# Turning k by a DMA transfer instead of TensorE, in a fused attention and MoE kernel

## The chip, the cores and the metric

The kernel runs on one core of one Trainium2 chip. The metric is the device time of one execution in microseconds (us); lower is better. Times of a kernel are given as the median of several runs with the lowest and highest.

## What is computed

Attention with a softmax that has one more term in its sum, over 8 batches, 12 heads, 448 rows and 64 columns of a head, and behind it a two-layer network with the Mish function on 3584 rows of 768:

```python
batch, n_heads, seq, head_dim = (8, 12, 448, 64)
n_tokens, d_model, d_ff = (3584, 768, 2048)

scores = scale * np.matmul(q, k.transpose(0, 1, 3, 2))
m = np.max(scores, axis=-1, keepdims=True)
e = np.exp(scores - m)
attn = e / (np.sum(e, axis=-1, keepdims=True) + np.exp(-m) + 1e-09)
attn_out = np.matmul(attn, v)
x = attn_out.transpose(0, 2, 1, 3).reshape(B * S, H * D)
h = x @ w_in
sp = np.where(h > 20.0, h, np.log1p(np.exp(np.minimum(h, 20.0))))
out = (h * np.tanh(sp)) @ w_out
```

All inputs and the output are float32 in HBM. The kernel multiplies in bfloat16.

## The kernel before

**Tiling.** Two heads of a batch make a pair, so there are 48 pairs, six a batch. Three pairs make a unit (`UNIT_PAIRS = 3`), and two units a batch. One pair takes 448 rows of q, k and v, held as 112 partitions times 4 rows (`SP_ = 112`, `NT = 4`).

**A pair's path.** `load_pair` (L121) brings q, k and v of a pair into float32 tiles, each by a transfer of 224 KB on the queue of SP (L128); each of the three has three buffers. `cast_pair` (L165) turns q and k into bfloat16 on GpSimd (L179, L180), `cast_v` (L185) does so for v (L188). `transpose_pair` (L190) turns q and k with TensorE: four transposes of 112x128 each for q and for k (L208), into two PSUM banks of a score tile. `evac_qk` (L221) copies them to SBUF: VectorE writes the scaled q in a block-diagonal tile `qd` in two halves (L254), ScalarE copies k to `kT` (L262). `scores` (L291) multiplies `qd` and `kT` into one of three score tiles (L311), and VectorE takes the row maximum `negm` (L332). `exps` (L337) runs the exponentials on ScalarE into `en` (L345). `denominators` (L363) and `normalise` (L410) scale `en` on VectorE (L414, seven a pair) and then turn it by one DMA transpose a pair on the queue of SP into `eT` (L422): 128 partitions times 28 blocks of 128 columns, 896 KiB. `av_pair` (L445) multiplies `eT` with v (L462), three pairs later than the pair's scores. A few early pairs have part of this turned by TensorE instead (L434).

**The network.** `mm1_mish` (L493) is one of 16 column blocks of the first layer for a batch: six matmuls (L498) and a Mish on ScalarE (L504). `mm2_part` (L523) makes parts of the second layer (L551), with a copy to `o_sb` on VectorE (L534) and stores on the queue of SP (L516).

**The order of the work.** It is written out by hand: each engine runs its instructions in program order, and so does the queue of SP. After six pairs done one by one (L618 to 651), the loop at L653 goes through the units, from u = 2. A unit has two stretches. The first (L664 to 717) has twelve steps: the exponentials of a step, a piece of the second layer as filler for TensorE, the scores ahead of it, and the AV product of the unit before at the end of each pair. At steps 0, 3 and 6 (`LOAD_AT`) it calls loads and casts:

```python
load_pair(at + LEAD, "qk")       # LEAD = 4 pairs ahead
load_pair(at + 1, "v")
cast_pair(at + LEAD - 1, with_v=False)
cast_v(at)
```

The second stretch (L724 to 746) has eight blocks f of the first layer. At f = 0 the unit's first pair is normalised and turned, at f = 3 and f = 7 the other two. At f = 1, 3 and 5 q and k of the next unit's three pairs are turned and copied (L740, L741). At f = 4, 6 and 7 the next unit's first scores are computed (L738, L743).

Loads, stores and the DMA transposes of `en` share the queue of SP, in program order: a unit's nine loads and its stores, then its three transposes. Each transfer also waits until the eighth transfer ahead of it on this queue has landed.

Of the kernel before, what the change touches and what calls it, by code (L numbers as in the profile page):

```python
# [10 lines left out]
BF16 = mybir.dt.bfloat16  # L11
# [4 lines left out]
UNIT_PAIRS = 3  # L16
# [3 lines left out]
def kernel(  # L20
# [9 lines left out]
    nc = tc.nc  # L30

    B, H, S, D = q.shape
# [3 lines left out]
    NT = 4  # L36
    SP_ = S // NT
    HP = H // 2
# [9 lines left out]
    N_PAIRS = B * HP  # L48
# [4 lines left out]
    def pool(name, bufs, space=None):  # L53
        if space is None:
            return ctx.enter_context(tc.tile_pool(name=name, bufs=bufs))
        return ctx.enter_context(tc.tile_pool(name=name, bufs=bufs, space=space))
# [2 lines left out]
    singles = pool("singles", 1)  # L59
    ld_pool = pool("ld", 3)  # L60
    bf_pool = pool("bf", 4)
    qk_pool = pool("qk", 3)
    st_pool = pool("st", 5)
    hl_pool = pool("hl", 4)
    rb_pool = pool("rb", 2)
# [38 lines left out]
    loaded, casted, qkT, att, xT, o_sbs, stats = {}, {}, {}, {}, {}, {}, {}  # L104
# [60 lines left out]
    def cast_pair(p, with_v=True):  # L165
        if p >= N_PAIRS:
            return
        q_f, k_f, v_f = (loaded[p].get(nm) for nm in "qkv")
        q_bf = bf_pool.tile([SP_, NT, 2, D], BF16, tag="q_bf", name="q_bf")
        k_bf = bf_pool.tile([SP_, NT, 2, D], BF16, tag="k_bf", name="k_bf")  # L170
        v_bf = bf_pool.tile([SP_, 2, NT * D], BF16, tag="v_bf", name="v_bf", bufs=12)
        by_t = "p h (t d) -> p t h d"
        q_t, k_t = (t.rearrange(by_t, t=NT) for t in (q_f, k_f))
        if p == 0:
            nc.vector.tensor_copy(out=k_bf, in_=k_t)
            for half in (slice(0, NT // 2), slice(NT // 2, NT)):
                nc.vector.tensor_copy(out=q_bf[:, half], in_=q_t[:, half])
        else:
            nc.gpsimd.tensor_copy(out=q_bf, in_=q_t)  # L179
            nc.gpsimd.tensor_copy(out=k_bf, in_=k_t)  # L180
        casted[p] = (q_bf, k_bf, v_bf)
        if with_v:
            cast_v(p)

    def cast_v(p):  # L185
        if p >= N_PAIRS:
            return
        nc.gpsimd.tensor_copy(out=casted[p][2], in_=loaded.pop(p)["v"])  # L188

    def transpose_pair(p, bank=None):  # L190
        if p >= N_PAIRS:
            return
        q_bf, k_bf, _ = casted[p]
        if bank is None:
            ps = mo_take()
            ps_k = mo_take() if p == 0 else ps
        else:
            ps, ps_k = sc_tiles[2 - bank][:, 0, :], sc_tiles[2 - bank][:, 1, :]
        by_s = [
            t[:, :].bitcast(BF16).rearrange("p (s n) -> p s n", s=2)[:, s, :]  # L200
            for s, t in enumerate((ps, ps_k))
        ]
        by_2 = sc_tiles[2][:, 0, :].bitcast(BF16)
        srcs = list(enumerate((q_bf, k_bf)))
        for s, src in reversed(srcs) if p == 0 else srcs:
            for t in range(NT):
                to = by_2 if p == 0 and s == 0 and t >= NT // 2 else by_s[s]
                nc.tensor.transpose(  # L208
                    to[:, t * SP_ : (t + 1) * SP_],
                    src[:, t].rearrange("p h d -> p (h d)"),  # L210
                    ident[:SP_, :SP_],
                )
        own = [] if bank is not None else [ps, ps_k] if p == 0 else [ps]
        qkT[p] = (by_s, own)
# [6 lines left out]
    def evac_qk(p, act=False):  # L221
        if p >= N_PAIRS:
            return
        (q_ps, k_ps), own = qkT[p]
        mo_free.extend(own)
        q_reads = []
        qd = q_diag[p % 3]
        kT = qk_pool.tile([128, S], BF16, tag="kT", name="kT")
        if p < DIAG_FROM:
            qT = qd.rearrange("d i h r -> d (i h r)")[:, 0:S]  # L230
            qkT[p] = (qT, kT)
            if p == 0:
                nc.scalar.copy(kT, k_ps[:, 0:S])
                by_2 = sc_tiles[2][:, 0, :].bitcast(BF16)
                for ps, half in (q_ps, slice(0, S // 2)), (by_2, slice(S // 2, S)):
                    nc.vector.tensor_scalar(
                        out=qT[:, half], in0=ps[:, half], scalar1=SCALE, scalar2=None,
                        op0=ALU.mult,
                    )
                return  # L240
            if act:
                nc.scalar.mul(qT, q_ps[:, 0:S], SCALE)
            else:
                q_reads.append(nc.vector.tensor_scalar(
                    out=qT, in0=q_ps[:, 0:S], scalar1=SCALE, scalar2=None, op0=ALU.mult
                ))
        else:
            qkT[p] = (qd, kT)
            if p < DIAG_FROM + 3:
                nc.vector.memset(qd[0:64, :, 1, :], 0.0)  # L250
                nc.vector.memset(qd[64:128, :, 0, :], 0.0)
            for h in range(2):
                rows = slice(64 * h, 64 * h + 64)
                q_reads.append(nc.vector.tensor_scalar(  # L254
                    out=qd[rows, :, h, :],
                    in0=q_ps[rows, 0:S].rearrange("d (i r) -> d i r", i=QB),
                    scalar1=SCALE, scalar2=None, op0=ALU.mult,
                ))
        if own and not act:
            nc.vector.tensor_copy(out=kT, in_=k_ps[:, 0:S])  # L260
        else:
            k_read = nc.scalar.copy(kT, k_ps[:, 0:S])  # L262
            if not own:
                apart(k_read, *q_reads)
# [145 lines left out]
    def normalise(p, dma=True):  # L410
# [9 lines left out]
        if dma:  # L420
            n = NT - 1 if p < HEAD else NT
            nc.sync.dma_start_transpose(  # L422
# [168 lines left out]
    LEAD = UNIT_PAIRS + 1  # L591
    LOAD_AT = (0, 3, 6)
    HEAD = HP

    BY_PE = {HEAD - 1: 1, HEAD: -2, HEAD + 1: 2}
    AV_AT = {0: {1: 3, 5: 4, 8: 5}, 1: {1: 8, 4: 6, 8: 7}}
# [20 lines left out]

    for p in range(HEAD):  # L618
        for s in range(STEPS):
# [33 lines left out]
    for u in range(UNITS_PER_B, N_UNITS + 2 * UNITS_PER_B):  # L653
# [10 lines left out]
        for n in range(steps):  # L664
            pi, s = divmod(n, STEPS)
            p, idx = p0 + pi, p0 * STEPS + n
            late_tp = u == UNITS_PER_B and n == STEPS
            exps(idx)
            if u == UNITS_PER_B + 1 and n == 0:
                for j in range(2):  # L670
                    turn_on_pe(HEAD, j, busy_first=3)
            flush_late()
            if late_tp:
                transpose_pair(p0 + 2)
                evac_qk(p0 + 2)
            if held and n == 1:
                late.extend(held)
                held.clear()
                flush_late()
            late.extend(slow)  # L680
            slow.clear()
            acc += weight[n]
            want = int(total * acc / sum(weight) + 1e-6)
            while done < want:
                fn, w = filler.popleft()
                fn()
                done += w
            scores_ahead(end)
            if n in LOAD_AT:
                at = p0 + LOAD_AT.index(n)  # L690
                load_pair(at + LEAD, "qk")
                load_pair(at + 1, "v")
                cast_pair(at + LEAD - 1, with_v=False)
                cast_v(at)
            for pe, n0 in BY_PE.items():
                j = n - n0
                first = 2 if pe == HEAD else 0
                if pe // UNIT_PAIRS == u - 1 < first_mm2 - 1 and first <= j < NT:
                    turn_on_pe(pe, j, busy_first=1)
            spread = RDEN_AT.get(u - UNITS_PER_B, {})  # L700
            if n in spread:
                on_act = u < first_mm2
                spread_rden(
                    spread[n], copy=nc.scalar.copy if on_act else nc.vector.tensor_copy,
                    behind=slow if on_act else late,
                )
            early = AV_AT.get(u - UNITS_PER_B)
            if early is not None and n == 7:
                keep_busy(6, bank=mo_free[0])
            if early is not None:  # L710
                if n in early:
                    av_pair(early[n], half=p)
            elif s == (2 if pi else 0) and N_PAIRS <= p < N_PAIRS + UNIT_PAIRS:
                av_pair(p - UNIT_PAIRS)
            if u - UNITS_PER_B < len(W_AT):
                at = (u - UNITS_PER_B, n)
                load_w(W_AT[at[0]].get(n, 0), behind=W_BEHIND.get(at))
# [6 lines left out]
        for f in range(FF_U):  # L724
# [19 lines left out]
            if f in (3, FF_U - 1) and p0 >= LATE_DIV:  # L744
                p = todo[1 + f // (FF_U - 1)]
# [33 lines left out]
```

## Time and profile before

| | |
|---|---|
| three runs, median (lowest to highest) | 480.35 us (479.74 to 483.63) |
| the profiled execution, its own time | 479.66 us |
| its span, first to last instruction | 477.9 us |
| granted TensorE clock, mean | 0.996 |
| busy: TensorE, VectorE, ScalarE, GpSimd | 458.8, 358.7, 344.7, 103.8 us |
| k turned by TensorE, all pairs | 192 transposes; ScalarE's copies of it at L262 from score tiles 20.8 us, 39 of 534 ns |
| DMA transposes of `en` | 45, median 6.7 us from issue to landing |
| loads of k | 48, median 5.2 us from issue to landing |

A busy time is the union of an engine's instructions; matmuls overlap in the array, so the time that one of them adds is the distance between two starts and not its own duration. A name such as "PE mo L551" is engine, tile written and source line. The rows of the DMA issues are those of the queue in which SP stands; the duration of such a row is how long SP was held by the issue, and the landing is told apart from it. SP has no row in the busy times.

### The profile page before, as it was taken

How to read it: one execution, taken by the hardware profiler on the slowest of the kernel's cores; microseconds unless marked ns; L12 is line 12 of the kernel's file. 1: busy time of each engine (PE TensorE's matmuls, PEld its weight loads, DVE VectorE, ACT ScalarE, POOL GpSimd, SP SyncE). 2: the span in 40 equal slices, each digit the busy share in tenths (PEclk: the TensorE clock that was granted, in tenths of full speed). 3: DMA queues.
4: the chain of work that ended last, by engine and by line, in shares of the span. 5: the costliest groups of instructions: out<-in, count | busy, mean ns of one | idle time of the engine just before them, and what ended most of it. 6: DMA issues, size and time to landing. Idle time of an engine off the chain costs nothing.

```text
span 477.9 us, 9363 instructions
## 1 busy us (share of the span) xinstructions
PE 458.8 (96%) x3291; PEld 257.8 (54%) x3291; DVE 358.7 (75%) x715; ACT 344.7 (72%) x907; POOL 103.8 (22%) x186
## 2 busy tenths in 40 slices
PE   6878999999999999999999999999999999999996
PEld 3344555555555565556555555555555555556563
DVE  5899849569898998889899979888898889421011
ACT  5998878788797868788787968687887978312300
POOL 3623536106031311304040312204040300000000
PEclk9999999999999999999999999999999999999999
DMA  8999999999999979898989999989989596961122
GB/s 215 227 224 213 234 222 183 185 212 233 195 301 207 261 149 214 211 198 227 192 229 171 267 156 260 198 192 231 190 220 198 173 181 156 156 142 34 34 63 71
DMA packets 204975, 91.09 MB, mean 191 GB/s; under 512 B 161792, under 2 KB 201472, under 8 KB 204928
## 3 DMA queue, kind: packets, MB, share of 16 engines
q1 hardware_dynamic: 197408, 84.18, 81.0%
q0 software_dynamic: 7488, 6.29, 8.8%
q8 instruction: 26, 0.43, 0.4%
q14 instruction: 21, 0.17, 0.1%
q10 hardware_dynamic: 32, 0.02, 0.0%
HBM read 45.61 MB, written 11.01 MB: 118 GB/s over the span
## 4 chain that ended last, share of the span: by engine, by line
PE 69%; DVE 8%; ACT 6%; issue 1%; DVEq 0%
PE mo L498 24%; PE mo L551 24%; PE sc L311 7%; ACT en L345 6%; PE sc L462 6%; DVE negm L332 5%; PE sc L498 3%; PE sc L208 3%; DVE en L414 1%; DVE xT L475 1%; PE mo L462 1%; DVE o_sb L534 1%; PE mo L272 0%; DVE eT L437 0%; ACT L345 0%
## 5 line engine op out<-in xcount | busy, mean ns | idle before, releaser
L345 ACT ACTIVATE en<-sc,negm 128x448 bf16<-128x448 f32 x336 | 208.7, 640 | 22.5 <-DVE negm L332 20.7
L332 DVE TENSOR_REDUCE negm<-sc 128x2 f32<-128x896 f32 x192 | 182.6, 970 | 39.6 <-PE sc L311 29.3
L551 PE MATMUL mo<-w_out_sb,gT 128*128 128x384 bf16 (+1 forms) x1024 | 166.8, 307 | 0.4 <-DVE rb L402 0.4
L498 PE MATMUL mo<-xT,w_in_sb 128*128 128x448 bf16 x672 | 141.9, 353 | 0.3 <-DVE xT L475 0.3
L551 PEld LDWEIGHTS <-gT 128*128 128x128 bf16 x1024 | 96.3, 98 | 56.0 <-issue 1.9
L504 ACT ACTIVATE gT<-mo 128x448 bf16<-128x448 f32 x112 | 59.3, 543 | 78.9 <-PE mo L498 78.6
L498 PEld LDWEIGHTS <-w_in_sb 128*128 128x128 bf16 x768 | 72.7, 98 | 63.4 <-issue 3.2
L179 POOL CAST q_bf<-q_f 112x512 bf16<-112x512 f32 x47 | 29.9, 635 | 222.1 <-DMA q_f<-in_q_dram 196.1
L414 DVE TENSOR_SCALAR en<-en,rden 128x448 bf16<-128x448 bf16 x252 | 74.2, 367 | 0.8
L311 PE MATMUL sc<-kT,qd 128*128 128x448 bf16 x252 | 71.6, 354 | 0.1
L345 ACT ACTIVATION_READ_ACCUMULATOR en<-sc,negm 128x1 f32 x336 | 71.0, 211 | 0.0
L534 DVE COPY o_sb<-mo 128x384 f32<-128x384 f32 (+1 forms) x64 | 31.8, 497 | 48.3 <-PE mo L551 48.1
L462 PE MATMUL sc<-eT,v_bf 112*64 112x448 bf16 x336 | 39.8, 357 | 1.4 <-ACT en L345 0.9
L311 PEld LDWEIGHTS <-qd 128*128 128x128 bf16 x252 | 24.4, 97 | 29.0 <-issue 12.9
L188 POOL CAST v_bf<-v_f 112x512 bf16<-112x512 f32 x48 | 29.9, 624 | 31.5 <-DMA v_f<-in_v_dram 31.4
L254 DVE TENSOR_SCALAR qd<-sc 64x448 bf16<-64x448 bf16 x72 | 27.7, 385 | 6.2 <-PE sc L208 5.4
L462 PEld LDWEIGHTS <-v_bf 112*64 112x64 bf16 x384 | 20.0, 109 | 20.0 <-issue 11.6
L180 POOL CAST k_bf<-k_f 112x512 bf16<-112x512 f32 x47 | 29.2, 622 | 6.1 <-DMA k_f<-in_k_dram 3.5
L262 ACT COPY kT<-sc 128x448 bf16<-128x448 bf16 x39 | 20.8, 534 | 0.6 <-PE sc L208 0.6
L498 PE MATMUL sc<-xT,w_in_sb 128*128 128x448 bf16 x96 | 20.8, 353 | 0.0
L475 DVE CAST xT<-sc 128x448 bf16<-128x448 f32 x33 | 20.3, 614 | 0.0
L208 PEld LDWEIGHTS <-q_bf 112*128 112x128 bf16 x192 | 13.7, 99 | 10.0 <-POOL q_bf L179 2.0
(61 smaller groups left out, 278.9 us busy)
## 6 DMA issues: line engine op xcount, KB each, us to landing
k_f<-in_k_dram SPq DMA_DIRECT2D x48, 224.0 KB, 5.2
q_f<-in_q_dram SPq DMA_DIRECT2D x48, 224.0 KB, 5.2
v_f<-in_v_dram SPq DMA_DIRECT2D x48, 224.0 KB, 5.5
w_in_sb<-in_moe_w_in_dram POOLq DMA_DIRECT2D x12, 256.0 KB, 8.7
w_out_sb<-in_moe_w_out_dram POOLq DMA_DIRECT2D x8, 384.0 KB, 10.1
out_dram<-o_sb SPq DMA_DIRECT2D x7, 336.0 KB, 3.7
out_dram<-o_sb SPq DMA_DIRECT2D x8, 288.0 KB, 4.8
out_dram<-o_sb SPq DMA_DIRECT2D x8, 240.0 KB, 3.4
```

The source lines that it names most:

```text
L179: nc.gpsimd.tensor_copy(out=q_bf, in_=q_t)
L180: nc.gpsimd.tensor_copy(out=k_bf, in_=k_t)
L188: nc.gpsimd.tensor_copy(out=casted[p][2], in_=loaded.pop(p)["v"])
L311: nc.tensor.matmul(sc[:, bk, 0:S], lhsT=qT[:, i].rearrange("d h r -> d (h r)"), rhs=kT, start=True, stop=True,)
L332: half_max[p] = nc.vector.tensor_reduce(out=negm, in_=sc[:, 0 : len(cols), 0:S], axis=AX.X, op=ALU.max, negate=True)
L345: e = nc.scalar.activation(out=st["en"][:, :, c, 0:SP_], in_=sc[:, bk, 0:S].rearrange("q (j c) -> q j c", j=NT), func=AF.Exp, bias=st["neg ...
L414: nc.vector.tensor_scalar(out=en[:, :, i, 0:SP_], in0=en[:, :, i, 0:SP_], scalar1=st["rden"][:, i : i + 1], scalar2=None, op0=ALU.mult,)
L462: mm = nc.tensor.matmul(av[h * 64 : (h + 1) * 64, 0:S], lhsT=v_bf[:, h, j * D : (j + 1) * D], rhs=e_h, start=(j == 0), stop=(j == NT - 1),)
L498: nc.tensor.matmul(h_ps[:, 0:S], lhsT=w_in_sb[:, dm, ff * 128 : (ff + 1) * 128], rhs=xT[b][:, dm, :], start=(dm == 0), stop=(dm == DM_T - 1),)
L504: nc.scalar.activation(out=gT[:, ff, b % 2 * S : b % 2 * S + S], in_=h_ps[:, 0:S], func=AF.Mish)
L534: nc.vector.tensor_copy(out=o_sb[:, cols.start : cols.start + n_dve], in_=st["o"][:, 0:n_dve])
L551: nc.tensor.matmul(st["o"][:, 0:n_cols], lhsT=gT[:, ff, i * 128 : (i + 1) * 128], rhs=w_out_sb[:, ff, cols], start=(ff == 0), stop=(ff == ...
```

## The change

From pair 15 on (`K_BY_DMA_FROM = 2 * HP + UNIT_PAIRS`), k is turned by a DMA transpose on the queue of SP. It is issued right behind the cast of that pair's k in the order of the program, so between the loads of the unit before: behind the three loads of steps 0, 3 and 6, once each. It reads the cast tile (112 partitions times 512) and writes `kT` (128 partitions times 4 blocks of 112), which the scores read. TensorE then turns q alone for these 33 pairs (15 to 47), and ScalarE makes no copy for them. `kT` gets six buffers where it had three. The tile of v's cast is taken when v is cast instead of when q and k are, and has eight buffers where it had twelve. By the two programs' orders, TensorE has 132 transposes and their weight loads fewer, ScalarE 33 copies fewer, the queue of SP 33 transfers more; VectorE and GpSimd have the same instructions in the same order.

```diff
-    qk_pool = pool("qk", 3)
+    qk_pool = pool("qk", 6)
...
-        q_f, k_f, v_f = (loaded[p].get(nm) for nm in "qkv")
+        q_f, k_f = (loaded[p][nm] for nm in "qk")
...
-        v_bf = bf_pool.tile([SP_, 2, NT * D], BF16, tag="v_bf", name="v_bf", bufs=12)
...
-        casted[p] = (q_bf, k_bf, v_bf)
+        casted[p] = [q_bf, k_bf, None]
...
-        nc.gpsimd.tensor_copy(out=casted[p][2], in_=loaded.pop(p)["v"])
+        v_bf = bf_pool.tile([SP_, 2, NT * D], BF16, tag="v_bf", name="v_bf", bufs=8)
+        nc.gpsimd.tensor_copy(out=v_bf, in_=loaded.pop(p)["v"])
+        casted[p][2] = v_bf
+
+    kT_ahead = {}
+
+    def turn_k_by_dma(p):
+        if not K_BY_DMA_FROM <= p < N_PAIRS:
+            return
+        kT_ahead[p] = qk_pool.tile([128, S], BF16, tag="kT", name="kT")
+        nc.sync.dma_start_transpose(
+            out=kT_ahead[p].rearrange("d (t p) -> d t p", t=NT),
+            in_=casted[p][1].rearrange("p t h d -> p (t h d)"),
+        )
...
-        srcs = list(enumerate((q_bf, k_bf)))
+        srcs = list(enumerate((q_bf, k_bf)))[: 1 if p in kT_ahead else 2]
...
-        kT = qk_pool.tile([128, S], BF16, tag="kT", name="kT")
+        kT = kT_ahead.pop(p, None)
+        by_dma = kT is not None
+        if not by_dma:
+            kT = qk_pool.tile([128, S], BF16, tag="kT", name="kT")
...
+        if by_dma:
+            return
         if own and not act:
             nc.vector.tensor_copy(out=kT, in_=k_ps[:, 0:S])
         else:
...
+    K_BY_DMA_FROM = 2 * HP + UNIT_PAIRS
...
                 cast_pair(at + LEAD - 1, with_v=False)
+                turn_k_by_dma(at + LEAD - 1)
                 cast_v(at)
```

## The prediction, made before the changed kernel ran

> **What bounds the kernel now.** I read the page's busy times first, then the chain that ended last, then one period of the unit loop in sums per stretch, then the timelines of TensorE and SP inside it.
>
> ```profile
> PE 458.8 (96%) x3291; PEld 257.8 (54%) x3291; DVE 358.7 (75%) x715; ACT 344.7 (72%) x907; POOL 103.8 (22%) x186
> ...
> PE 69%; DVE 8%; ACT 6%; issue 1%; DVEq 0%
> ```
>
> TensorE works for 96% of the span and carries 69% of the chain. The first AV products of successive units start at 153.2, 179.7, 206.2, 232.8, 259.2 and so on to 391.8, so a unit takes 26.5 us. Two such periods in sums (columns: length, then busy time and instructions of TensorE, weight loads, VectorE, ScalarE, GpSimd, then clock, DMA share, GB/s):
>
> ```profile
> 206.20:232.80 26.60, 26.50 (x192) 15.63 (x193) 23.66 (x49) 21.56 (x57) 5.62 (x9) 1.00 0.95 212
> 232.80:259.20 26.40, 26.40 (x174) 14.31 (x173) 23.80 (x48) 21.48 (x57) 5.44 (x9) 1.00 0.91 207
> ```
>
> TensorE has no idle time in a period, at full clock; VectorE needs 23.2 of it in the mean over nine periods, ScalarE 21.5. So inside the loop time is worth what it takes from TensorE. The chain in order of time, in the stretch of the first layer, says what the transposes take there (start, us, what):
>
> ```profile
> 248.46 1.14 PE mo L498 x6
> 249.59 0.40 PE sc L208 x8
> 249.99 1.14 PE mo L498 x6
> 251.12 0.38 PE sc L311 x2
> ```
>
> Eight transposes (four of q, four of k) hold the chain for 0.40 us between two groups of matmuls. TensorE's timeline of a later unit shows the halves: k's start 0.20 us behind q's, and the next matmul 0.20 us behind k's. Each row's 0.36 us is mostly overlap.
>
> ```profile
> 273.27 0.36 PE L208 MATMUL sc<-ident,q_bf 112*128 112x112 bf16 x4
> 273.47 0.36 PE L208 MATMUL sc<-ident,k_bf 112*128 112x112 bf16 x4
> 273.67 1.30 PE L498 MATMUL sc<-xT,w_in_sb 128*128 128x448 bf16 x6
> ```
>
> **Removed.** 33 pairs times 0.20 us of TensorE is 6.6 us, all on the path as long as TensorE has no idle time: 0.6 us in each of 11 units (those whose second stretch turns pairs 15 to 47). It cannot be more than the rows' union of 0.36 us a pair, 11.9 us, and I take 0.20 because the distance of starts is what the next instruction sees. The 33 copies of ScalarE at 534 ns are 17.6 us, and worth nothing: in that stretch ScalarE waits for TensorE (the waits have 78.6 us of Mish at L504 behind L498), and a period would have to fall from 26.5 to about 21 before ScalarE bound it.
>
> **Added on the queue of SP.** 33 transposes, each 112x512 bfloat16 = 112 KiB, an eighth of a transpose of `en` (896 KiB). The rows for the price of an issue:
>
> ```profile
> L422 SPq DMA_TRANSPOSE eT<-en x31: 4099/4246/5017, 127.8 to 391.6; - x31
> ...
> DMA to landing us min/median/max: 6.1/6.6/8.4
> ```
>
> (ns, fewest, median, most). An eighth of 4.25 is 0.53; with the semaphore I take 0.6 us. From below, the issue of a plain load of 224 KB holds SP 0.41 us. From above: in the first 50 us the transposes of 21 blocks held SP at least 4.02 us, hardly less than 28 blocks, so a fixed cost near 4 us is not excluded by durations alone. What speaks for the eighth is that bytes flow at a steady 216 to 218 GB/s during an issue (the windows 252 to 253 and 254 to 255 us), and 896 KiB at that rate are 4.2 us: SP is held as long as the bytes take. The 21-block ones ran beside weight loads.
>
> SP's own time in a period is visible in its timeline:
>
> ```profile
> 196.24 14.65 SPq L422 DMA_TRANSPOSE eT<-en  x3
> 211.00 0.98 SPq L516 DMA_DIRECT2D out_dram<-o_sb  x2
> ...
> 217.17 1.80 SPq L516 DMA_DIRECT2D out_dram<-o_sb  x2
> 222.96 4.13 SPq L422 DMA_TRANSPOSE eT<-en  x1
> ```
>
> Over 196.24 to 222.96 the issues of three transposes (13.1), nine loads and four stores add up to 18.7 us, semaphores 0.3; SP waits for the other 7.7, and 5.6 to 8.1 in the steady periods. Into this go three issues (1.8 us) and the waits for casts. The first `kT` of a unit finds its k cast long ago. The second waits for a k whose load was issued three issues earlier: in the unit at 264, that k's cast ends at 269.4, where SP would stand at about 267.9, so 1.5 us; the third about 0.5 us. Behind these waits stand the next loads, the stores and the next unit's three transposes of `en`. In all 3.8 us of 7.4 (6.8 when a period is 0.6 shorter): it fits, and costs 0. On the page of the Trainium skill "VectorE: DVE Perf Modes", section "The three transpose paths", a 128x128 transpose is given as 390 ns on TensorE and 1309 ns by DMA, and its section "Rules for kernel authors" says to use TensorE if PSUM may take the result. By these figures four blocks would be an estimated 5.2 us of DMA against 1.6 us of TensorE, and the change would lose. The trace differs from both: 28 blocks in 4.25 us are 152 ns a block, and a transpose on TensorE adds 50 ns.
>
> **Added on the DMA engines.** 112 KiB at 217 GB/s are 0.53 us, at the 290 GB/s seen in other windows 0.40. From above, add the spread of the landings of `en`'s transposes, 8.4 less 6.1, for transposes that meet other traffic: 2.8 us. I take 1.0, near the lower end, as 0.53 plus half a microsecond for each change from copies to a transpose and back. Three a period are 3 us. The cover: the DMA engines stand still before a unit's first transpose of `en` (0.00 in the windows 249 to 251 and 275 to 276, 1 to 2 us), and each such transpose flows at SP's 218 GB/s where 290 is possible, 1.0 us of reserve each. That is about 4.5 us. What is late next is `eT`: it lands 1.9 to 5.2 us before its AV product in the steady units, median 3.4 (the transpose issued at 254.55 lands at 260.6, its AV starts at 264.2). Only in the first changed unit is there less: issue 123.40, landing 131.4, AV 131.6, with weight loads in the queue. There I put 0.5 us of stall (bounds 0 and 1.5).
>
> **Moved waits.** `qd` on VectorE does not get faster: TensorE reaches the scores at f = 4 0.4 us earlier and those at f = 7 0.6 us earlier. In 9 of 11 units `qd` is ready 0.4 to 1.9 us ahead. In two it is not (118.40 and here), and there the 0.6 us are lost:
>
> ```profile
> 250.89 0.17 PEld L311 LDWEIGHTS <-qd 128*128 128x128 bf16 x2 [0.20 <-DVE qd L254]
> ```
>
> Two times 0.6 is 1.2 us back (bounds 0, and 6.6 if VectorE holds every unit). `kT` itself is issued near 266.5 in this unit and read at 277.5; no wait. GpSimd's cast of k now waits for the `kT` of four pairs before, a unit earlier: nothing. v's eight buffers cover the five or six pairs alive. Buffers of `kT`: six, for two units.
>
> **Sum.** 6.6 less 1.2 less 0.5 is 4.9. Span 477.9 less 4.9 is 473.0, plus the 1.76 between the profiled execution's span and its time (479.66) is 474.8. The median of the runs is 0.69 above that execution: **475.4 us**, 1.0% under 480.35. With one to one and a half microseconds on the waits either way, 474.4 to 476.4.
>
> **Rivals.**
>
> - *All of it counts.* VectorE and `eT` keep up everywhere: 480.35 less 6.6 is 473.7. For it: most units have slack in `qd` and `eT`. Against: 250.89 and 131.4 above. Chance 0.18.
> - *Hidden by VectorE.* It has 23.2 of 26.5 us of work and holds 8% of the chain; if its lag carries from unit to unit, a third of the 6.6 stays: 478.2 (476.4 to 480.4). Against: ScalarE and TensorE have the same first stretch as before, and the next exponential starts 2.4 us or more behind its maximum at a unit's start. Chance 0.17.
> - *The DMA engines become the bound* (the other side). A period's DMA work is at least 26.5 less 1.5 still less 3.0 reserve, 22.0 us. With `kT` at c each, 22.0 + 3c passes the new period of 25.9 at c = 1.3 and the old one of 26.5 at c = 1.5: from there `eT` lands late in every unit and TensorE waits at L462. At c = 1.9 a period is 27.7, 1.2 above before, times ten: 492. At the upper bound 2.8 it is 30.4: 519. For it: the DMA share is 0.91 to 0.99 in most periods; `kT` sits among loads, where a mix of copies and transposes landed late before (8.0 us for the one issued at 123.40). Against: the reserve above. Chance 0.22, from 484 up mostly.
> - *A fixed issue cost.* Each `kT` holds SP about 4 us: 18.7 + 0.3 + 12 is 31.0 us a period, 4.5 above, times 11: 530. It decides from 1.6 us an issue ((7.4 less 0.6 less 2.0)/3). The page cited above comes out on this side too. Against: bytes and issue go in step. Chance 0.06.
>
> That the change does not do what it says is excluded by the two programs' orders: 132 transposes are gone and 33 transfers are there.
>
> **How the numbers follow.** Forecast 0.37. A measurement of this kernel tells about 1% from no change, 4.8 us. Faster by that (under 475.55): the first rival's 0.18 and 0.22 of the forecast. Within 1%: 0.15 of the forecast, 0.17 hidden, 0.04 of the DMA case near its point. Slower: 0.18 and 0.06. The range 473.0 to 486.0 leaves out the fixed cost (0.06), the DMA case above 486 (0.12) and 0.02 below.
>
> **What would show it.** L208 with 60 transposes of k where it had 192; the copies of L262 from score tiles 6 where there were 39. The period between first AV products: 25.9 in most units. The new issues near 0.6 us and landing about 5 us later; their waits 1 to 2 us on GpSimd's cast. `eT` landing no more than 1.5 us later against its AV. What would make me wrong: TensorE waiting at L462 for `eT` (DMA), issues of 1.6 us and more, or L311 waiting for L254 in every unit.

## The result and the profile after

The changed kernel takes 482.73 us (median of 22 runs, 480.19 to 485.64), the kernel before 480.08 us in the 22 runs beside it (478.86 to 483.63). The ratio is 1.0056, with an interval from 1.0035 to 1.0076. So the change costs about half a per cent. The forecast was a gain of 1%; its range holds the time, its sign is wrong. The profiled execution took 482.76 us with a span of 481.0 us at a mean granted clock of 0.985. All lines of `kernel.py` behind the new function stand 12 to 17 lines lower: AV is now L479, the scores L328, the transposes of `en` L439, those of q L220, `qd` L269, and the new transposes of k are L197.

The page, its busy times and the chain by engine and by line:

```profile
PE 457.1 (95%) x3159; PEld 252.2 (52%) x3159; DVE 362.0 (75%) x715; ACT 332.0 (69%) x874; POOL 104.2 (22%) x186
...
PE 56%; DVE 12%; ACT 9%; DMA 7%; issue 1%; SPq 0%; DVEq 0%
PE mo L568 20%; PE mo L515 18%; ACT en L362 8%; DMA eT<-en 6%; PE sc L328 6%; PE sc L479 6%; DVE negm L349 5%; DVE en L431 4%; PE sc L515 3%; DVE qd L269 2%; PE sc L220 1%; PE mo L479 1%; ACT L362 1%; DVE xT L492 1%; PE mo L289 0%
```

TensorE has 132 instructions fewer and ScalarE 33, as the change says. New is `DMA eT<-en` with 6% of the chain: the transposed `en` was never on it before. TensorE's share falls from 69% to 56% because the chain leaves TensorE for what was late.

Successive periods from the first AV product of a unit to the next (columns as before: length, then busy time and instructions of TensorE, weight loads, VectorE, ScalarE, GpSimd, then clock, DMA share, GB/s):

```profile
183.60:209.60 26.00, 26.00 (x162) 13.79 (x161) 23.29 (x47) 20.39 (x54) 5.58 (x9) 1.00 1.08 227
209.60:237.20 27.60, 26.11 (x178) 15.00 (x177) 24.04 (x50) 21.76 (x60) 5.50 (x9) 1.00 1.07 215
237.20:263.60 26.40, 26.01 (x163) 13.82 (x165) 23.47 (x48) 19.34 (x50) 5.59 (x9) 1.00 1.04 223
```

TensorE needs 26.0 us of a period where it needed 26.5. The first of the three has that length. The second is 27.60 us with 1.49 us of idle TensorE, and the third has 0.39. In the two periods shown of before it had 0.1 us or none. Over the nine periods from 157.7 to 395.0 us the lengths add up to 237.3 us and TensorE's work to 233.7, so 3.6 us are idle. What it waits for stands in its timeline at the end of the second period:

```profile
232.67 3.43 PE L568 MATMUL mo<-w_out_sb,gT 128*128 128x192 bf16 x28
237.21 0.95 PE L479 MATMUL sc<-eT,v_bf 112*64 112x448 bf16 x8 [1.10 <-DMA eT<-en]
```

It waits for `eT` at AV. That row is a unit's first AV, and in the stretch from 145 to 400 us there are four such waits of TensorE (3.3 us in all) and four of its weight loads (4.2 us, partly at the same times). Before there were none. The first layer's stretch of the chain has what the change removed (start, us, what):

```profile
223.84 0.20 PE sc L220 x4
224.04 1.14 PE sc L515 x6
```

Four transposes of q take 0.20 us of the chain where eight of q and k took 0.40.

The new transfers as one line's instructions (ns: fewest, median, most):

```profile
L197 SPq DMA_TRANSPOSE kT<-k_bf x33: 1183/1192/2215, 106.2 to 384.0; - x33
...
DMA to landing us min/median/max: 3.0/4.1/10.0
```

An issue holds SP for 1.19 us. The transposes of `en` in the steady stretch from 145 to 400 us, first before the change and then after it:

```profile
L422 SPq DMA_TRANSPOSE eT<-en x30: 4099/4246/5017, 143.4 to 391.6; - x30
L422 SPq EVENT_SEMAPHORE  x29: 28/1071/6422, 147.8 to 389.7; - x29
```

```profile
L439 SPq EVENT_SEMAPHORE  x30: 27/28/444, 149.1 to 394.2; - x30
L439 SPq DMA_TRANSPOSE eT<-en x30: 4131/4308/5503, 149.2 to 394.7; - x30
...
DMA to landing us min/median/max: 6.1/6.5/8.4
```

The row of semaphores is how long SP stood in front of such a transpose. Before, half of them were waited for by 1.07 us and more, up to 6.4: SP was there first, and `en` came later. After, SP never stands for more than 0.44 us: `en` is there first, and SP comes late. The landing is told from the issue, and at 6.1 to 8.4 us it is what it was before. In the nine steady units from 153 to 395 us `en` is written as early as before (16.3 us behind the unit's first AV product in the mean). The unit's first `eT` is issued 2.0 us behind that writing where it was 0.07, and it travels 6.9 us where it was 6.4. So `eT` is late mainly because its transfer starts late; the longer way adds half a microsecond in the mean, and 2.1 us in the period shown next (8.3 against 6.2).

SP's timeline of the period in which TensorE waited shows what fills the queue:

```profile
215.64 0.99 SPq L533 DMA_DIRECT2D out_dram<-o_sb  x2
216.68 0.43 SPq L128 DMA_DIRECT2D q_f<-in_q_dram  x1
217.15 1.23 SPq L128 DMA_DIRECT2D k_f<-in_k_dram  x1
218.42 0.46 SPq L128 DMA_DIRECT2D v_f<-in_v_dram  x1
219.32 1.18 SPq L197 DMA_TRANSPOSE kT<-k_bf  x1
...
222.84 1.20 SPq L197 DMA_TRANSPOSE kT<-k_bf  x1
...
226.44 1.19 SPq L197 DMA_TRANSPOSE kT<-k_bf  x1
227.73 0.99 SPq L533 DMA_DIRECT2D out_dram<-o_sb  x2
228.82 14.35 SPq L439 DMA_TRANSPOSE eT<-en  x3
```

In the corresponding period before, SP had done its stores by 218.97 and stood until 222.96, where `en` came: the first `eT` was issued 16.7 us behind the first AV of the unit (206.22). Here it is 19.2 us behind it (209.64), directly behind the stores. SP does not wait longer for the eighth transfer ahead: it is idle in front of the nine loads for 0.4 us a period now and was for 1.1.

### The profile page after: what moved, and what is told of

Same layout as the page of the kernel before. It is cut to its first block, busy times and chain, and to the rows that moved or that the text cites. A ratio compares the mean times of both kernels' runs of the same rounds, so it can differ in the third digit from the quotient of the medians.

```text
span 481.0 us, 9077 instructions
## 1 busy us (share of the span) xinstructions
PE 457.1 (95%) x3159; PEld 252.2 (52%) x3159; DVE 362.0 (75%) x715; ACT 332.0 (69%) x874; POOL 104.2 (22%) x186
## 4 chain that ended last, share of the span: by engine, by line
PE 56%; DVE 12%; ACT 9%; DMA 7%; issue 1%; SPq 0%; DVEq 0%
PE mo L568 20%; PE mo L515 18%; ACT en L362 8%; DMA eT<-en 6%; PE sc L328 6%; PE sc L479 6%; DVE negm L349 5%; DVE en L431 4%; PE sc L515 3%; DVE qd L269 2%; PE sc L220 1%; PE mo L479 1%; ACT L362 1%; DVE xT L492 1%; PE mo L289 0%
## 5 line engine op out<-in xcount | busy, mean ns | idle before, releaser
L431 DVE TENSOR_SCALAR en<-en,rden 128x448 bf16<-128x448 bf16 x252 | 79.1, 385 | 0.8
L328 PE MATMUL sc<-kT,qd 128*128 128x448 bf16 x252 | 71.9, 355 | 1.1 <-DVE qd L269 1.0
L479 PE MATMUL sc<-eT,v_bf 112*64 112x448 bf16 x336 | 40.5, 362 | 6.7 <-DMA eT<-en 3.3
L328 PEld LDWEIGHTS <-qd 128*128 128x128 bf16 x252 | 24.6, 98 | 31.2 <-issue 15.8
L188 POOL CAST v_bf<-v_f 112x512 bf16<-112x512 f32 x48 | 29.9, 624 | 25.8 <-DMA v_f<-in_v_dram 25.4
L479 PEld LDWEIGHTS <-v_bf 112*64 112x64 bf16 x384 | 20.0, 110 | 25.9 <-issue 11.7
L179 POOL CAST k_bf<-k_f 112x512 bf16<-112x512 f32 x47 | 29.4, 626 | 12.5 <-DMA k_f<-in_k_dram 11.9
L269 DVE TENSOR_SCALAR qd<-sc 64x448 bf16<-64x448 bf16 x72 | 27.7, 385 | 3.9 <-PE sc L220 3.1
L220 PEld LDWEIGHTS <-q_bf 112*128 112x128 bf16 x192 | 13.8, 99 | 9.6 <-POOL q_bf L178 1.4
```

The lines of the kernel that those rows point to most:

```text
L188: nc.gpsimd.tensor_copy(out=v_bf, in_=loaded.pop(p)["v"])
L269: q_reads.append(nc.vector.tensor_scalar(out=qd[rows, :, h, :], in0=q_ps[rows, 0:S].rearrange("d (i r) -> d i r", i=QB), scalar1=SCALE, sc ...
L328: nc.tensor.matmul(sc[:, bk, 0:S], lhsT=qT[:, i].rearrange("d h r -> d (h r)"), rhs=kT, start=True, stop=True,)
L431: nc.vector.tensor_scalar(out=en[:, :, i, 0:SP_], in0=en[:, :, i, 0:SP_], scalar1=st["rden"][:, i : i + 1], scalar2=None, op0=ALU.mult,)
L479: mm = nc.tensor.matmul(av[h * 64 : (h + 1) * 64, 0:S], lhsT=v_bf[:, h, j * D : (j + 1) * D], rhs=e_h, start=(j == 0), stop=(j == NT - 1),)
```

## What it could be, and the experiments

Four explanations are told apart. The saving on TensorE may be smaller than 6.6 us, or VectorE may take it back. The queue of SP may be too full: its issues, its waits for casts and the order of its transfers make `eT` start late. The DMA engines may be too full, whatever the order. And the first changed unit, in which the loads of the network's weights still run, may be the only one that pays. Each kernel below was timed in five rounds against the kernel before, and its ratio is to that.

**1. Only TensorE's part.** From pair 15 on nothing turns k and no transfer takes its place; the scores of all later pairs read the `kT` of pair 14. The kernel leaves out the turning of k for pairs 15 to 47. Its buffers are those of the changed kernel, so they cost nothing that shows.

```diff
+    kT_last = singles.tile([128, S], BF16, tag="kT_last", name="kT_last")
...
-        kT_ahead[p] = qk_pool.tile([128, S], BF16, tag="kT", name="kT")
-        nc.sync.dma_start_transpose(
...
+        kT_ahead[p] = kT_last
...
+            if p == K_BY_DMA_FROM - 1:
+                kT = kT_last
```

> The saving alone: from pair 15 on nothing turns k (the scores of later pairs read pair 14's turned k, so k is left out of them), no transposes of k on TensorE, no copy on ScalarE, no transfer on SP's queue. Theory Q (the transfers on SP's queue make eT late and TensorE waits for it; the 6.6 us of TensorE are real): 473.5 to 475.5 us, ratio to before 0.986 to 0.991, periods of 25.9 us. Rival V (VectorE takes the time back whatever SP does): 478 or more, ratio 0.995 or above, TensorE waiting for the maximum or for qd in every unit.

Measured: 474.14 us (472.66 to 475.10), ratio 0.988 (0.9861 to 0.9900), 5.8 us less than the 479.93 beside it. Two periods of it:

```profile
187.90:213.80 25.90, 25.79 (x166) 14.01 (x166) 22.70 (x49) 20.38 (x54) 4.97 (x9) 1.00 0.92 207
213.80:240.40 26.60, 26.23 (x177) 14.70 (x177) 24.54 (x50) 20.27 (x53) 7.05 (x12) 1.00 0.97 219
```

Five of nine periods are 25.9 us, and the others 26.1 to 26.6, as the second. So 5.8 of the 6.6 us are real, and VectorE does not take them back. The changed kernel is 8.6 us slower than this one: that is the price of the 33 transfers. By the third AV product of each unit (profiled executions, from 110 us to the last unit) the changed kernel loses 3.7 us in the first changed unit (29.5 against 25.8) and 3.7 us in the ten others (264.6 against 260.8).

**2. Only the transfers.** TensorE and ScalarE turn and copy k as before, and the 33 transfers write a tile that nothing reads. (`kT` has fewer buffers in kernels 2, 5 and 6: three, four and three.)

```diff
-        kT_ahead[p] = qk_pool.tile([128, S], BF16, tag="kT", name="kT")
+        spare = qk_pool.tile([128, S], BF16, tag="kT_spare", name="kT_spare")
...
-            out=kT_ahead[p].rearrange("d (t p) -> d t p", t=NT),
+            out=spare.rearrange("d (t p) -> d t p", t=NT),
```

> The added transfers alone: TensorE and ScalarE turn and copy k as before, and the 33 DMA transposes write a tile that nobody reads. Theory Q: slower, 483 to 488 us, ratio 1.007 to 1.016; eT lands 0 to 2 us before its AV product instead of 2 to 5, the first changed unit loses most. Rival V: 480, ratio 0.998 to 1.002. Issue of a transpose held SP 1.19 us in the changed kernel, expected again.

Measured: 483.66 us (480.24 to 485.70), ratio 1.0075 (1.0052 to 1.0098). The transfers cost 3.7 us even when TensorE leaves them more time. Its profiled execution was the quickest of its runs, so where the 3.7 us lie in a typical one is not seen.

**3. From pair 21 on**, when the loads of the weights are over: the change to `K_BY_DMA_FROM = 21`, 27 pairs.

```diff
-    K_BY_DMA_FROM = 2 * HP + UNIT_PAIRS
+    K_BY_DMA_FROM = 21
```

> The change from pair 21 on instead of 15, so that no unit with weight loads has a DMA transpose of k. Theory Q1 (about half of the loss is the collision with the weight loads at 116 to 135 us, where eT landed 128.8 and the AV products slipped by 3 us against before): 27 pairs save 5.4 us and steady units lose 2 to 4: 476.5 to 479, ratio 0.992 to 0.998. Theory Q2 (the loss is spread evenly over the units): ratio 1.003 to 1.006.

Measured: 479.68 us (477.11 to 482.24), ratio 0.9996 (0.9976 to 1.0015), between what the theories said. Beside the changed kernel 3.1 us come back with the two units left alone, though these two also give up 1.2 us of saving. But nine units that should save 0.6 us each, 5.4 in all, save nothing: SP stands 0.1 us in front of the first `eT` in every unit, as in the changed kernel. Both losses exist, at the start and in each unit.

**4. The loads of v off SP's queue.** The changed kernel, with the loads of v of later pairs issued on GpSimd's queue; this frees SP of three issues a period.

```diff
-            nc.sync.dma_start(
+            queue = nc.gpsimd if nm == "v" and p > K_BY_DMA_FROM else nc.sync
+            queue.dma_start(
```

> The changed kernel with the loads of v from pair 16 on issued by GpSimd's queue instead of SP's: the same bytes, three issues of 0.5 us a unit fewer on SP. Theory S (the time SP is held is what makes eT late): eT's slack grows by 1 to 2 us, 477 to 480 us, ratio 0.994 to 1.000. Theory D (the DMA engines are what is full): no change against the changed kernel, ratio 1.004 to 1.008.

Measured: 495.89 us (490.23 to 497.25), ratio 1.0314 (1.0271 to 1.0356). No theory had that. The timelines of SP and of GpSimd show a load that starts inside an `eT`:

```profile
257.05 15.88 SPq L440 DMA_TRANSPOSE eT<-en  x3
```

```profile
258.24 0.66 POOL L129 DMA_DIRECT2D v_f<-in_v_dram  x1
```

The `eT` issued at 257.05 lands at 267.83, 10.8 us behind its issue, and the load issued at 258.24 lands at 267.55. On SP's queue a load is issued only when SP is done with the issue of the transpose ahead; from GpSimd's queue it starts 1.2 us behind the transpose here. From 110 us on each `eT` holds SP for 5.2 us in the mean instead of 4.7, and a unit's first one takes 9.8 us to land in the nine steady units instead of 6.9. So the overlap goes with a loss in this run, and the question for which it was made is not answered.

**5. One block instead of four.** As 1, with a transfer at each of the 33 places that turns one of k's four blocks into a tile that nothing reads. Pairs 15 to 47 have no k of their own, as in 1.

```diff
-        kT_ahead[p] = qk_pool.tile([128, S], BF16, tag="kT", name="kT")
+        kT_ahead[p] = kT_last
+        spare = qk_pool.tile([128, SP_], BF16, tag="kT_spare", name="kT_spare")
...
-            out=kT_ahead[p].rearrange("d (t p) -> d t p", t=NT),
-            in_=casted[p][1].rearrange("p t h d -> p (t h d)"),
+            out=spare, in_=casted[p][1][:, 0].rearrange("p h d -> p (h d)")
```

> The saving as in the kernel where nothing turns k (474.1 us, the scores of later pairs read pair 14's turned k), plus, at each place of a DMA transpose of k, one of a single block of 112 columns by 128 where the change has four, into a tile that nobody reads. If the price of a transfer of k is its bytes on the DMA engines, a quarter of the 8.6 us between the changed kernel and that one is left: 476 to 477. If it is the time that an issue holds SP and the waits for casts between the loads, an issue here holds SP about 1.0 us, nearly the 1.19 of four blocks, and the time is 479 to 483.

Measured: 478.50 us (476.12 to 481.42), ratio 0.9969 (0.9947 to 0.9992). It lies between the two expectations. Against kernel 1 the transfer of a quarter of the bytes still costs 4.4 of the 8.6 us.

```profile
L199 SPq DMA_TRANSPOSE kT_spare<-k_bf x33: 1092/1116/2082, 105.8 to 379.1; - x33
```

One block holds SP for 1.12 us and four for 1.19. Between one block and four the price of such an issue hardly depends on the size.

**6. A plain copy.** As 1, with a copy of the same 112 KiB at the same places, that does not transpose (pairs 15 to 47 have no k of their own).

```diff
-        nc.sync.dma_start_transpose(
...
+        kT_ahead[p] = kT_last
+        spare = qk_pool.tile([SP_, NT * 2 * D], BF16, tag="kT_spare", name="kT_spare", bufs=2)
+        nc.sync.dma_start(out=spare, in_=casted[p][1].rearrange("p t h d -> p (t h d)"))
```

> The same, with a plain copy of the same 112 KiB in SBUF at each of these places instead of a transpose: the same place, the same wait for the cast, an issue of about 0.5 us. If the transposing itself costs (an issue of 1.19 us, and an order among the DMA engines that copies don't need), 475 to 477. If the bytes or the waits for the casts cost, 480 to 483.

Measured: 478.31 us (474.46 to 486.38), ratio 0.9959 (0.9939 to 0.9980).

```profile
L199 SPq DMA_DIRECT2D kT_spare<-k_bf x33: 517/524/1105, 106.4 to 379.9; - x33
```

The copy holds SP for less than half as long, 0.52 us, and still costs 4.2 of the 8.6 us, again between the two expectations. Whether transposes need an order among the DMA engines, as was supposed, no run shows. So half of the price is paid by any transfer at these places of the queue, each with its wait for a cast. In the profiled executions the first changed unit of kernels 5 and 6 takes 28.7 and 28.3 us, which is 2.9 and 2.5 above kernel 1 where the changed kernel is 3.7 above it. The ten other units together are 1.1 us above in both, where the changed kernel is 3.7 above. So the loss at the start hardly depends on what is transferred, and the loss in the steady units goes with less of either, time or bytes. In both kernels SP stands only 0.1 us in front of most units' first `eT`, as in the changed one.

**7. Other places in the queue.** All bytes as in the changed kernel. A unit's first transfer stays behind the loads of step 0, the second goes behind the loads of step 6, and the third behind the next unit's first `eT`. So no transfer stands between two groups of loads except the first, and each finds its cast done.

```diff
-                turn_k_by_dma(at + LEAD - 1)
+                if n == LOAD_AT[0]:
+                    turn_k_by_dma(p0 + UNIT_PAIRS)
                 cast_v(at)
+                if n == LOAD_AT[2]:
+                    turn_k_by_dma(p0 + UNIT_PAIRS + 1)
...
+                turn_k_by_dma(p0 + UNIT_PAIRS + 2)
```

> The changed kernel with two of the three transfers of k moved on the queue of SP: the second of a unit behind the loads of step 6, where its cast is long done, the third behind the unit's first transpose of en. Same work, no waits for casts between loads, one transfer fewer ahead of the first transpose of en. If the waits and the place count: 477 to 480, ratio 0.993 to 1.000. If the sum of the time that SP is held or the DMA engines count: 482 to 484, ratio 1.004 to 1.008.

Measured: 478.75 us (476.97 to 482.48), ratio 0.9977 (0.9954 to 1.0000); 4.0 us less than the changed kernel, with the same transfers. The first changed unit still takes 28.4 us, 2.6 above kernel 1, so the new places help the units behind it more than this one.

**8. Other places, from pair 21 on.** As 7, with `K_BY_DMA_FROM = 21`.

> The same two moves, from pair 21 on, so no DMA transpose of k meets the weight loads: 474.5 to 477.5, ratio 0.988 to 0.995, if place and collision each cost what the runs so far suggest; 479 to 480 (as from pair 21 without the moves) if the place counts for nothing.

Measured: 476.77 us (475.89 to 478.18), ratio 0.9939 (0.9921 to 0.9957). Kernel 3 has the same 27 transfers and takes 479.68 us; the two intervals do not touch. One period of it, and its transposes of `en`:

```profile
189.20:215.10 25.90, 25.79 (x166) 14.00 (x167) 23.15 (x48) 20.36 (x54) 5.35 (x9) 1.00 1.04 219
```

```profile
L439 SPq DMA_TRANSPOSE eT<-en x30: 4117/4299/5581, 143.6 to 388.5; - x30
L439 SPq EVENT_SEMAPHORE  x30: 27/28/5866, 148.3 to 397.5; - x30
```

The periods are as long as those of kernel 1, 26.0 us in the mean, with the DMA share at 1.01 to 1.07. SP stands 1.0 to 2.7 us in front of the first `eT` in most units again, and the profile has no wait of TensorE for `eT` after 145 us. The DMA engines carry the same bytes in such a period without a loss, so in the steady units they were not at their limit: with the first order, SP got to `eT` too late.

**9. Only the first changed unit.** The changed kernel with the new path for pairs 15 to 17 alone.

```diff
-        if not K_BY_DMA_FROM <= p < N_PAIRS:
+        if not K_BY_DMA_FROM <= p < K_BY_DMA_FROM + UNIT_PAIRS:
```

> The change for pairs 15 to 17 alone, the unit whose transfers of k meet the last weight loads. If that meeting costs what the traces suggest (29.5 us from the AV product at 110.8 to that at 140.3, where the kernel with the saving alone has 25.8, and 26.6 before): 482 to 483.5, ratio 1.004 to 1.008, nearly all of the changed kernel's loss. If the loss is spread over all units: 480, ratio 0.999 to 1.001.

Measured: 481.42 us (480.15 to 487.53), ratio 1.0048 (1.0018 to 1.0078). The median is 1.1 us above the 480.30 beside it, a ratio of 1.0023 and below the 482 to 483.5 expected; the ratio given lies higher, and three of the twelve runs took 486.7 to 487.5 us. So three transfers in this unit cost more than the 0.6 us that they save; that they cost nearly as much as all 33 is not shown. Its timeline of TensorE:

```profile
127.41 0.95 PE L479 MATMUL sc<-eT,v_bf 112*64 112x448 bf16 x8 [1.11 <-DMA eT<-en]
```

**10. Other places, from pair 18 on.** As 7, with `K_BY_DMA_FROM = 18`, 30 pairs.

> The two moved transfers, from pair 18 on. If only the weight loads' unit is harmful: 475.5 to 476.7, a little under the same from pair 21 (476.77), ratio 0.990 to 0.994. If the unit behind it, with six stores, has no room either (AV products 1.7 us later in the kernel with the two moves from pair 15): 477 to 478.5, ratio 0.994 to 0.998.

Measured: 476.73 us (474.90 to 479.42), ratio 0.9930 (0.9902 to 0.9957). Pairs 18 to 20 add nothing that can be told from kernel 8.

**11. Behind the loads, ahead of `eT`.** As 8, but the third transfer beside the second, behind the loads of step 6.

```diff
                 if n == LOAD_AT[2]:
                     turn_k_by_dma(p0 + UNIT_PAIRS + 1)
+                    turn_k_by_dma(p0 + UNIT_PAIRS + 2)
```

> From pair 21 on; the second and third transfers of k both behind the loads of step 6, ahead of the first transpose of en. No wait for a cast between loads, but all three transfers are still ahead of that transpose. If the waits between the loads are what costs: 476.5 to 477.5, as with the third behind the first transpose of en (476.77). If what counts is how much of SP stands ahead of that transpose: 478.5 to 479.7, as without moves (479.68).

Measured: 477.88 us (476.15 to 480.56), ratio 0.9955 (0.9936 to 0.9974). It lies between kernels 3 and 8: of the 2.9 us between them about 1.8 go with taking the waits for casts from between the loads, and 1.1 with letting `eT` pass the third transfer. The intervals overlap, so the split is a tendency.

**12. One of three.** From pair 18 on, only the first pair of each unit takes the new path, at its old place.

```diff
-        if not K_BY_DMA_FROM <= p < N_PAIRS:
+        if p % UNIT_PAIRS or not K_BY_DMA_FROM <= p < N_PAIRS:
```

> From pair 18 on, by DMA only the first pair of each unit, at step 0, where its cast is long done: ten transfers, 2.0 us of TensorE saved. SP has 7 us idle a period for one issue of 1.2: 477.9 to 478.5, ratio 0.995 to 0.998, if nothing else is hit; 480 if even one transfer makes eT late.

Measured: 478.41 us (477.68 to 478.84), ratio 0.9955 (0.9942 to 0.9967). Ten transfers bring 1.9 us of the 2.0 that TensorE saves on ten pairs. In this kernel SP still stands 2.8 to 5.3 us in front of each unit's first `eT`: one transfer a period fits without any loss, three do not.

## Why the prediction was wrong

**Removed from TensorE: right.** 6.6 us were summed up, less 1.2 that VectorE takes back. Kernel 1 has 5.8 us less, so about 0.8 was kept. In its trace the waits of TensorE for another engine's result in the scores are for VectorE's `qd` (0.7 us from 145 to 400 us, and 2.2 of the weight loads). In the changed kernel its part is small too; the wait of the scores for `qd` is

```profile
  PE sc L328: 1.0, 3
```

three waits in the whole run. The rival in which VectorE hides the saving falls.

**The price of an issue on SP: mis-sized.** It was taken as 0.6 us, an eighth of the transpose of `en`, because bytes and issue went in step. That proportion holds for 28 blocks and not for four: 1.19 us, and 1.12 for one block (kernel 5). The bounds of 0.41 and 4.02 held it. But this price alone is not the failure: the copy of kernel 6 holds SP for 0.52 us, less than was forecast, and still costs 4.2 us, and kernels 3 and 8 differ by 2.9 us with issues of nearly the same price (1.28 and 1.24 us in the mean). The rule of the Trainium skill (page "VectorE: DVE Perf Modes", sections "The three transpose paths" and "Rules for kernel authors") is to use TensorE if PSUM may take the result; the change as made, which goes against it, lost. Its 1309 ns for one block by DMA is near the 1.12 us that one block of 112x128 holds SP here; the 1.19 us of four show that it can't be multiplied by the blocks. And the rule does not hold for kernels 8 and 10, which turn k by DMA and win.

**"It fits, and costs 0": the step that failed.** The forecast put 3.8 us into 6.8 us of waiting time of SP in a period (7.4 less 0.6). Measured over eight periods, from the first `eT` issued at 149.2 us to that at 361.6 (143.4 to 355.6 before), the three issues come to 3.7 us. The other issues got longer too, for which the forecast had nothing: the three transposes of `en` from 4.35 to 4.55 us in the mean, 0.6 us together, and the copies, 12.5 in the mean period, from 0.46 to 0.55, 1.0 us. So SP's issues grew by 5.3 us, from 18.9 to 24.2 us a period. The waits for casts, taken as 2.0, stand in this row:

```profile
SPq L197 <- POOL v_bf L188: 15.7, 13, 2.4
```

The row counts to the end of the cast that it names, the one that GpSimd did next to the one of k, and so says too much: SP's idle time in front of the three `kT` is 1.3 us a period. With 1.0 us of small gaps between its instructions and 0.1 in front of the unit's first `eT`, SP now needs 26.5 us, the whole period, where 25.9 was forecast. Of the waiting time before, 4.2 us lay in front of that `eT`. The predicted point from which a fixed issue decides, 1.6 us, was too high for the same reason: with the waits, longer issues and gaps as measured it is an estimated 1.0 us ((6.8 less 3.9)/3). The rival of a fixed issue cost had the kind right, as one block costs nearly what four do, and its size of 4 us wrong.

**What is late next: named rightly, judged wrongly.** The forecast named `eT`, with a median of 3.4 us between landing and AV. It is 1.4 us now in the steady units, and 0.2 us or less in front of five AV products there and the first one of the first changed unit. The expectation was "no more than 1.5 us later"; the median is 2.0 us later, and a unit's first is hit hardest, since it stands directly behind the loads and stores. This is the place of the rival "DMA engines become the bound", but not its cause in the steady units: the landing of `eT` still takes 6.5 us, and kernel 8 carries transfers of the same kind in these units without loss. The 1.0 us that the forecast gave each transfer on the DMA engines, half of it for the changes between copies and transposes, is measured by no run.

**The first changed unit: mis-sized.** It was given 0.5 us of stall, with bounds of 0 and 1.5. It costs 3.7 against kernel 1. SP's timeline, TensorE's timeline and the sums over a short stretch behind it, all of the changed kernel:

```profile
113.17 2.21 SPq L197 DMA_TRANSPOSE kT<-k_bf  x1
116.70 18.96 SPq L439 DMA_TRANSPOSE eT<-en  x3
```

```profile
128.82 1.63 PE L479 MATMUL sc<-eT,v_bf 112*64 112x448 bf16 x8 [2.05 <-ACT en L362]
```

```profile
128.90:132.30 3.40, 3.40 (x14) 1.30 (x15) 1.15 (x2) 0.60 (x2) 0.00 (x0) 0.50 1.12 208
```

Here SP was not late: the `eT` was issued 0.06 us behind the writing of its `en`, as before. But it holds SP for 9.86 us where that of the kernel before held it for 5.59, and lands at 128.77, 12.1 us behind its issue, where it took 7.7 before and 7.5 in kernel 1. So this loss is in the transfer itself, on the side of the rival of the DMA engines, and not in SP's order. The row of TensorE names ScalarE as what ended the wait; the landing 0.05 us ahead of the start shows that it was the transfer. From 116.9 to 125.8 loads of weights land too, the unit's last loads at 117.2 to 120.6 (before the change by 114.2, ahead of the issue of `eT`), and the `kT` issued at 113.17 only at 123.19. The stall is 2.05 us. Then TensorE's clock is granted at 0.50 for 3.41 us, and the third AV product of the unit comes 11.5 us behind the first instead of 9.9: 1.6 us more. Kernel 9 fits this place; in its profiled run the stall is 1.1 us and the clock stays at 1.00, so the size differs from run to run.

**The sum, corrected.** 6.6 less 0.8 is 5.8; less 3.7 in the first unit, less 3.7 in the others, less 1.2 that the medians of the changed kernel and of kernel 1 differ beyond these (8.6 against 7.4) gives 2.8 us slower. Of the 1.2, 0.5 lies ahead of 110 us in the two profiled runs, and the profiled run of kernel 1 was 0.7 above its median. Measured are 2.65. As the 8.6 us are the difference of two medians, the sum must come out; it says where the time lies and is no proof of the causes. That the range of 473.0 to 486.0 holds the time is no merit of the forecast's mechanism, which gave 474.4 to 476.4; the range reached up for the rivals.

**What stays open.** How much of the price in the steady units is SP's time and how much the engines' is not settled. Kernel 5 has fewer bytes at the same hold, kernel 6 less hold at the same bytes, and each gives back about half; so the bytes count beside the hold, and the two were not parted. At the start, where weights, loads and transposes meet, it is open which of them makes the first `eT` so long: it takes 12.5 us with a quarter of k's bytes (kernel 5), 11.0 with a copy (kernel 6) and 10.6 at the other places (kernel 7). Kernel 4 was meant to part SP's time from the engines' and brought an effect of its own. Why the clock fell to a half behind one stall and not behind others was not tried; the length of the stall does not decide it, as 2.05 us in the changed kernel had it and 2.39 us in kernel 5 had not.

## What to carry to other kernels

Before work is moved to a DMA queue, add up the time that each of its issues holds the engine that issues it, and price a small transposing transfer by a small one (here 1.12 to 1.19 us) and never by a share of a large one. Then ask what stands behind it in the queue: a transfer that waits for its input, put ahead of one on which the busiest engine depends, uses up what the queue has in reserve, here about 7 us a period with 4.2 of them in front of that transfer. The same 27 transfers gave nothing at the first places tried and 0.6% at better ones, so the place decides as much as the price.

## What the runs showed of the hardware

- A DMA transpose issued by SP held it for 1.12 us with one block of 112x128, 1.19 us with four, and 4.25 us with 28 of 128x128. A plain copy of the four blocks' bytes held it for 0.52 us.
- Loads of 224 KB issued on GpSimd's queue, so that they overlap with transposes on SP's, went with such a transpose landing 10.8 us behind its issue in the case shown, where 6.5 is the median in the changed kernel; the kernel lost 3.1%.
- A stretch of 3.41 us with TensorE's clock at 0.50 stood behind TensorE's wait of 2.05 us at 128.8 us in the changed kernel, and one of the same length at 131.7 us in kernel 4 behind a wait of 4.98; one of 6.83 us began in kernel 4 at 377.4 us inside a wait of 4.65. Behind waits of 1.1 us in kernel 9, 2.39 in kernel 5 and 2.43 in kernel 4 there is none.
